# Keys laid out tile by tile, with more transposes given to the DMA and a new order of instructions

## The chip, the cores and the metric

The kernel runs on one core of a Trainium2 chip. Its time is the device time of one execution in microseconds (us); before the change the median of three runs is 264.69 us (263.86 to 265.36). The profile is one execution, recorded by the hardware profiler; its span is 262.8 us from the first instruction to the last. The engines are called by what they do: TensorE (PE in the profile; its weight loads are PEld) multiplies matrices, VectorE (DVE) and ScalarE (ACT) compute elementwise and read its results, GpSimd (POOL) computes elementwise on the on-chip memory, and SyncE (SP, with its queue SPq) issues transfers. Each engine takes its instructions strictly in the order in which the program has them.

## The reference, cut to what matters

Attention over 4 batches, 8 heads, 768 positions and 64 elements per head. Three heads see all earlier positions; the other five see only the last 64 positions and the first 4. The attention output is then the input of a gated feed-forward block.

```python
scores = (1 / sqrt(D)) * q @ k^T                      # [4, 8, 768, 768]
stream_keep = causal & (is_sink | in_win)             # n_sink 4, window 64
mask = where(is_retrieval, causal, stream_keep)       # heads 0, 2, 6 are retrieval
a = exp(where(mask, scores, -1e9) - max); a = a / sum(a)
x = (a @ v) as [3072, 512]                            # batch and position by head and element
g = x @ w_gate; val = x @ w_val                       # 512 -> 1536
out = (g * sigmoid(g) * val) @ w_out                  # 1536 -> 512
```

## The kernel before

All matrices are float16 with float32 sums. Positions go in tiles of 128; a *pair* is two tiles of one batch (12 pairs, 24 tiles), and the feed-forward block works on *groups* of four tiles (6 groups). Per pair the kernel loads q, k and v (512 KB each), casts them, and turns q and k so that the head's elements lie on the partitions. Per tile it computes scores (line 530), their exponentials (540), masks (548), the product with the values (560) and the division (577), and turns the result, `xb`, into `xt`. Per group and block of 128 columns there are a gate product and a value product (761), a tanh (767), two VectorE steps (771, 778), and per tile an output product in three parts (790).

Turning is done in two ways, and three constants say from which pair or tile on the second is used:

```python
XBAR = 12    # outputs: tiles 12 to 23 by a transposing DMA, earlier ones on TensorE
XQK = 5      # queries: pairs 5 to 11 by DMA
XK = 8       # keys:    pairs 8 to 11 by DMA
```

Keys on TensorE take eight transposes into a PSUM tile (line 423) and a copy out of it (lines 175 and 177, through a helper); by DMA they take four transfers for a pair:

```python
kT = [const.tile([128, 4, S], FH, name=f"kT{n}") for n in range(2)]   # by batch: element, head pair, position

def dmak(n, j):                                   # line 408; j: even or odd positions
    b, pi = QP[n]
    for m in range(2):                            # m: which tile of the pair
        at = pi * 256 + m * 128 + j * 64
        nc.sync.dma_start_transpose(
            out=kT[b % 2][:, :, at:at + 64],
            in_=hqs[n][m * 64:(m + 1) * 64, 1, j].rearrange("p r x -> p (r x)"))

def transposes(n, w):                             # w: 0 queries, 1 keys
    ...
    for j in range(2):
        for p in range(4):
            nc.tensor.transpose(tr[:, p, :, j, :] if w else tr[:, j, p, :],
                hqs[n][:, w, j, p // 2, (p % 2) * 128:(p % 2 + 1) * 128], ident)

def evack(n, x, ps):
    b, pi = QP[n]
    copy(T_ev[n, 2][x], kT[b % 2][:, ps, pi * 256:(pi + 1) * 256],
         trs[n, 1][:, ps].rearrange("c p m j n -> c p (m j n)"))
```

An output tile takes four transposes and a copy, or one transfer; a query pair takes two transfers of `hqz`, which holds the cast queries among zeros:

```python
def xtranspose(t):
    ...
    if t >= XBAR:
        nc.sync.dma_start_transpose(              # line 587
            out=xts[g][:, :, n * 128:(n + 1) * 128], in_=xb.rearrange("p a b d -> p (a b d)"))
        return
    ...
    for p in range(4):
        nc.tensor.transpose(tr[:, p, :], xb[:, p].rearrange("p a d -> p (a d)"), ident)   # line 593

def dmaq(n, j):                                   # line 400
    nc.sync.dma_start_transpose(
        out=qT[n % 2][:, :, :, j].rearrange("c s p n -> c (s p) n"),
        in_=hqz[:, j].rearrange("p s a x -> p (s a x)"))
```

The order of all instructions is planned ahead: `ORDER` is a string with two characters for each task, `WAYS` says which engine does a task that several could do. A number from 3700 on in `ORDER` is no task: it puts that many matmuls of the identity with itself there, which fill a gap of TensorE (`warm`).

```python
for number in P.order():
    if number < P.FILL:
        P.tasks[number].run()
    else:
        warm(number - P.FILL)
```

Of the kernel before, what the change touches and what calls it, by code (L numbers as in the profile page):

```python
# [13 lines left out]


ORDER = (
    "08020409001L1Mxp1T1U011W1N1Oy21Y1V0B251X1Z0A1Q051a1t061p031u1q261b1c1d072D1P2G1e0C1n1f1g271R1r28"
    "1o1S0i2E2F1i1j1h1k2I1K1v0D0E0F2J2A2H1l2K2C1s2j0o2k2L1m1y1w1x1z222M0j112120232V0H2B24292N2O0p109T"
    "2W2p2q2P2r122Z9U2X2a2b2s2t2Y9J159K2Q132u2R2v2S2c2T9W9V3Q9d2d2e2U0I2x369L9e0G2h9X9f2y9M2i9N0l9n9o"
    "169i9j2w303W9k9p319q3X3G3H9r2z3R9g9h9s2m3Y9v2l9t9u9w1B0m9O9P3D0k3E9Q9R9S9Y9Z2n3Z3A9a3M323a3B9l3C"  # L20
    "331E9m2oACAD3b3c0s34359b9c0K3FAHAI3eAE3p3d370OAJ0JAM0q0L3I3J3f38391FAN3t189xAO2f3uAK494FAL9y4H3K"
    "9z0n3g3wAP3L3xAQA24G3j3kA3A7190t3TA84s3h3y3NA43S3i4z504A3l3mA01H4I4J413VA13n42AR3o0MA93q3U3O3PAW"
    "3z0R3v43AS44A5A61I403r4N3s2g45464OAUAT4KAV0rAX47480z1C4LAY4D0N4rAZAFAa0uAG5b4W4a4bBPBQBRBS4qAvAw"
    "BT4M4Q4RAA4E4CBFAB0x1D4B0v1J4dAxAyBGBH0wAz4eBU174x4m5i4gBVBWBe0y1G4S5jBX141ABhAb4cBY4h4P4y54Ac0Q"
    "4T0WAd55AeBfBg4UBK51Ag4V0b4X4iBi52BABB0P4j5aBo5758Ah4f0X0UBC5FBNBp4t5JBLAiBM4k530V5K0T5L5Z595ABD"
    "BOAj6m0S5MBE4lB55hBq5N4Y4Z4n4uB60aBIAlBJ5B6756Am5P5Q5CBrBs5D5EBZBa6AAk4w5g0hB76EAn6F5R5SAoB85s5t"
    "66BjBbBm5O6B4o5kAf4v4p5l5mAq656D7T5H5I5G5T5UAr5u5v5VBk5wAsBlBnB0At6C5W5cBc5XB1626G5d5nB97a5e0Z6u"
    "BdB35YCw5x7UB2B4CD6H0d5o6JCx5f6KCG6kCE5yBt6l6S6VAu6WCy5z69607V68CF7XBuBv6IBw6L6Y6Z6r0YCH616qCN6s"
    "5p5qCcByCdCI63ApCeCQ6M6hCOCP8gCJ0g7b6O7WCSCT6NCRBzC0C17RCU8f6PCfCgCVCW6b6c6XCL5r7SCr6n6Q6TCKCs6t"
    "CMD66RD70c6v6aBx7YC36d6wCmD8CzD0C47Z7n0fCu6x6e7oCtCvCXCYCZCnCo6f6y796g0e81CpCq8364Ca6z7kD96U6jDA"  # L30
    "6i6o75767lC57374D1C67mCbD2D37172DkDlDmEOD47q8h7C6p7pDaEPEQ7DChCiD57r707zCj82877ECkCl777F7G7H7u78"
    "E480E5C8C27K7LERES7IDb86DcC9Du7y7A7B7JDd7xE6CACB847cDp7MDe7d7eDBDCDnDqDr8588DD7N7sC7DoDx7tDv89Ds"
    "DwDtEEEFEGDE8BDFDfDg8CDy8K8D7O7PDh8ADiDjE77f7gE88N8O8cEHDG8Q8RDzEIE0E9E1EA7QEB8E8FEJEK8i7wEL7h8e"
    "8mCCDHDIDJE27i7jDL8TE38UDMDN8l7vECDODPEx8GEDFHEMFI8dFJ8j8kEyEzENDQDR8H8ZDVDWF2DXDYDZDSDT8P8nF08o"
    "F1ET8p8IFgF3DUF5F4FA8q8rF68J8MF7EUF8EVEWF99194Fh8LEs8VEY95FiFBFCFD978SEZEaEtEv8WEu8X98FKEwFEDK8v"
    "8wFL99Eb8Y8aFjFMFNFF8b8s8x968tFO8uFkEXEd8yFREeEnFGEoFeEp8z9092Ec9C9DEfEgFSFTEqErEh9A9BEi9E9FFbFU"
    "FVFc9GEjEk9H93FdFWFfFXFZFP9IFYGPFaFQElGSGjFlFmGQGRGkGlFnFoEmGTG5G6GmGZGaG7GKFqGLGMFpGnGbFrFsFtG8"
    "GtGuG9GUGVGWGNGOFvGvGcGyGdH1FwGwGzH0FxGxH2FyGAGBGCGFGGFuGIGHGJGeGfGDG0GgGEGhGiGXGoGYGpFzG1G2G3Gr"
    "H3H4GqGsH5G4H8H9HAHDH6H7HBHCHEHFHIHGHHHJHKHLHM"
)  # L40
WAYS = (
    "000000000000000000000000000000000000000000000000000000000000001020021121222210112011001222001011"
    "001000000000000000000000000001101200212120111100100000000010000000000100022220000101000001000000"
    "110000100000000011012221020010100000100000000010100000000000000002202120010000000100000020010000"
    "010000001000122120100010010010000000001010000000000000001221221200010000000000000000000102021221"
    "000000100000000001000100000000012002200220000001000000000001200000000000000000020200000000100000"
    "000000000021010221110000001001000000000001000000000010022010000000010000000000011000100100000000"
    "000000000000000000000000000000000000000000000000000000000000000000000000000000000000100000000010"
    "000000000000000000000000000000000000000000000000000000000000000000000000000000000000000000000000"
    "000000000000000000000000000000000000000000000000000010000000000000010000000000000000000000000000"  # L50
    "000000000000000000000000000000000000000000000000000000000000000000000000000000000000000000000000"
    "000000000000000000001000000000000000000000000000000000000000000000000000000000000000000000000000"
    "000010000100001000000"
)
# [51 lines left out]
def kernel(  # L106
# [66 lines left out]
    def copy(task, dst, src):  # L173
        if task.way == "ACT":
            nc.scalar.copy(out=dst, in_=src)  # L175
        else:
            ENG[task.way].tensor_copy(out=dst, in_=src)  # L177
# [179 lines left out]

    XBAR = 12  # L360
# [52 lines left out]

    def transposes(n, w):

        ring = "gv" if w and n < 2 else "tr"
        if w:
            tr = buf(ring, [128, 4, 2, 2, 64], FH, "tr")
        else:
            tr = buf(ring, [128, 2, 4, 128], FH, "tr")  # L420
        for j in range(2):
            for p in range(4):
                nc.tensor.transpose(
                    tr[:, p, :, j, :] if w else tr[:, j, p, :],
                    hqs[n][:, w, j, p // 2, (p % 2) * 128:(p % 2 + 1) * 128], ident)
# [482 lines left out]
```

The softmax here doesn't subtract the row's maximum and nothing guards it: scores larger than these inputs give would overflow.

## Time and profile before

| | |
|---|---|
| time, median of 3 | 264.69 us (263.86 to 265.36) |
| span of the profiled execution | 262.8 us |
| TensorE clock granted | 0.996 |
| moved by DMA | 41.23 MB, 157 GB/s in the mean |
| first real transpose on TensorE starts | 5.78 us |
| last matmul ends about | 258.3 us |

In the lists, an instruction stands with its line, its engine and `out<-in`; x is how often it comes, then follow its busy time, the mean of one in ns, and the time the engine stood idle just before it with what ended that wait. A matmul's mean contains its way through the array, which the next one overlaps, so that the means of small matmuls add up to more than they cost. The 40 slices of the page are 6.6 us each and count busy tenths. A line of the chain is work that nothing else could have replaced on the way to the last instruction, followed back from it.

### The profile page before, as it was taken

To read this page: it belongs to the slowest core of one execution; us is meant where nothing else is said; L and a number is where in the kernel's file an instruction comes from. 1 tells how busy PE (TensorE), PEld (TensorE's weight loads), DVE (VectorE), ACT (ScalarE), POOL (GpSimd) and SP (SyncE) were. 2 spreads that over 40 slices of the span, in tenths; PEclk is the share of its full clock that TensorE was granted. 3 is DMA by queue.
4 is the path that set the end of the run, shared out by engine and by line. 5 is a ranking of instruction groups with operands and counts; after the bars stand their busy time and mean duration, and the time that the engine had idled before them with its cause. 6 is when DMAs were issued, how large, how long until landed. Compare 5 with 4: busy or idle time off the path is not lost.

```text
span 262.8 us, 4993 instructions
## 1 busy us (share of the span) xinstructions
PE 247.6 (94%) x1890; PEld 141.3 (54%) x1890; DVE 174.6 (66%) x357; ACT 140.3 (53%) x216; POOL 89.7 (34%) x123
## 2 busy tenths in 40 slices
PE   7878899899999989999899999999999999999993
PEld 7656775565555655545455555554555554444441
DVE  3887988989777569857398747527459365557421
ACT  2777797686548467758286754722363522323100
POOL 5468769462268073261330033800315100000000
PEclk9999999999999999999999999999999999999998
DMA  6999999994999979794972342253212221211143
GB/s 185 302 275 329 326 312 310 319 361 124 219 290 291 228 196 147 184 237 101 263 119 60 43 99 58 55 120 69 62 40 62 62 58 40 47 36 41 28 94 81
DMA packets 75192, 41.23 MB, mean 157 GB/s; under 512 B 27552, under 2 KB 70560, under 8 KB 75168
## 3 DMA queue, kind: packets, MB, share of 16 engines
q1 hardware_dynamic: 75088, 40.78, 63.9%
q8 instruction: 15, 0.25, 0.4%
q10 hardware_dynamic: 80, 0.13, 0.2%
q14 instruction: 9, 0.07, 0.1%
HBM read 28.31 MB, written 6.29 MB: 132 GB/s over the span
## 4 chain that ended last, share of the span: by engine, by line
PE 67%; DMA 12%; DVE 6%; SPq 6%; POOL 3%; ACT 3%; issue 2%; POOLq 0%; DVEq 0%; ACTq 0%
PE gv L761 36%; PE o_ps L790 20%; PE sc L530 6%; DMA raw<-in_q_dram 6%; PE av L560 4%; DMA qT<-hqz 3%; DMA raw<-in_k_dram 3%; SPq L309 3%; SPq L400 2%; DVE sil L771 1%; DVE e L548 1%; ACT e L540 1%; POOL hq L177 1%; DVE h L778 1%; POOL e L548 1%
## 5 line engine op out<-in xcount | busy, mean ns | idle before, releaser
L540 ACT ACTIVATE e<-sc 128x1024 f16<-128x1024 f32 (+4 forms) x71 | 62.2, 879 | 41.0 <-PE sc L530 40.4
L761 PE MATMUL gv<-xt,wv_sb 128*128 128x512 f16 (+1 forms) x304 | 73.0, 368 | 1.0 <-DVE sil L771 1.0
L761 PE MATMUL gv<-xt,wg_sb 128*128 128x512 f16 (+1 forms) x304 | 72.9, 368 | 0.6 <-POOL wg_sb L177 0.6
L771 DVE SCALAR_TENSOR_TENSOR sil<-sig,gv 128x512 f32<-128x512 f32 (+1 forms) x76 | 49.4, 655 | 32.8 <-ACT sig L767 32.4
L790 PE MATMUL o_ps<-wo_sb,h 128*128 128x512 f16 x288 | 69.7, 379 | 0.0
L767 ACT ACTIVATE sig<-gv 128x512 f32<-128x512 f32 (+1 forms) x76 | 43.0, 574 | 45.1 <-PE gv L761 44.5
L778 DVE SCALAR_TENSOR_TENSOR h<-sil,gv 128x512 f16<-128x512 f32 (+1 forms) x76 | 49.3, 656 | 24.2 <-PE gv L761 23.0
L548 POOL TENSOR_TENSOR e<-e,m 128x1024 f16<-128x1024 f16 (+1 forms) x17 | 31.8, 1873 | 54.1 <-ACT e L540 54.0
L761 PEld LDWEIGHTS <-wv_sb 128*128 128x128 f16 x304 | 28.6, 98 | 28.0 <-issue 1.3
L761 PEld LDWEIGHTS <-wg_sb 128*128 128x128 f16 x304 | 28.5, 98 | 26.3 <-POOL wg_sb L177 0.8
L790 PEld LDWEIGHTS <-h 128*128 128x128 f16 x288 | 27.3, 98 | 28.5
L530 PE MATMUL sc<-qT,kT 128*128 128x256 f16 (+1 forms) x276 | 37.5, 257 | 3.1 <-DMA qT<-hqz 2.0
L530 PEld LDWEIGHTS <-kT 128*128 128x128 f16 x276 | 24.6, 98 | 15.7 <-DMA qT<-hqz 3.0
L560 PEld LDWEIGHTS <-e 128*128 128x128 f16 x472 | 20.2, 97 | 10.0 <-DVE vt L177 1.5
L560 PE MATMUL av<-vt,e 128*128 128x65 f16 x472 | 22.5, 193 | 1.7 <-DVE vt L177 1.0
L577 DVE TENSOR_TENSOR xb<-av,rc 128x256 f16<-128x256 f32 x48 | 20.2, 423 | 1.5
L177 POOL CAST vt<-raw 64x512 f16<-64x512 f32 x21 | 13.8, 660 | 11.1 <-DMA raw<-in_v_dram 10.3
L177 POOL CAST hq<-raw 128x1024 f16<-128x1024 f32 (+1 forms) x14 | 14.8, 1058 | 6.6 <-DMA raw<-in_q_dram 5.1
L548 DVE TENSOR_TENSOR e<-e,m 128x640 f16<-128x640 f16 (+1 forms) x21 | 15.8, 754 | 1.8 <-ACT e L540 1.7
L175 ACT COPY o_sb<-o_ps 128x512 f32<-128x512 f32 x15 | 8.8, 584 | 11.6 <-PE o_ps L790 11.6
L177 POOL COPY vt<-vt 2x330 f16<-2x330 f16 x20 | 9.6, 481 | 14.2 <-PE av L560 13.6
L177 DVE COPY o_sb<-o_ps 128x512 f32<-128x512 f32 x8 | 5.5, 690 | 9.3 <-PE o_ps L790 8.0
(59 smaller groups left out, 142.0 us busy)
## 6 DMA issues: line engine op xcount, KB each, us to landing
raw<-in_q_dram SPq DMA_DIRECT2D x12, 512.0 KB, 6.9
raw<-in_k_dram SPq DMA_DIRECT2D x12, 512.0 KB, 7.4
raw<-in_v_dram SPq DMA_DIRECT2D x12, 512.0 KB, 7.4
out_dram<-o_sb SPq DMA_DIRECT2D x47, 128.0 KB, 2.4
raw<-in_moe_w_gate_dram SPq DMA_DIRECT2D x6, 512.0 KB, 8.0
raw<-in_moe_w_val_dram SPq DMA_DIRECT2D x6, 512.0 KB, 7.5
raw<-in_moe_w_out_dram SPq DMA_DIRECT2D x6, 512.0 KB, 8.5
kT<-hq SPq DMA_TRANSPOSE x16, 2.5
```

The source lines that it names most:

```text
L175: nc.scalar.copy(out=dst, in_=src)
L177: ENG[task.way].tensor_copy(out=dst, in_=src)
L530: nc.tensor.matmul(sc[c // 4][:, c % 4:c % 4 + n, :], weights, moving, start=first, stop=last)
L540: nc.scalar.activation(out=e[:, 0:n], in_=whole_sc.pop((t, u))[:, 0:n], func=AF.Exp, scale=scale)
L548: ENG[task().way].tensor_tensor(out=ev, in0=ev, in1=mm, op=ALU.mult)
L560: nc.tensor.matmul(av[:, n, 0:65], ee, vv, start=(m == 0), stop=(m == len(bl) - 1))
L577: nc.vector.tensor_tensor(out=xbs[t][:, :, odd, :], in0=av[:, :, 0:64], in1=rc.to_broadcast([128, 4, 64]), op=ALU.mult)
L761: nc.tensor.matmul(ps, wsb[:, kk, j * 128:(j + 1) * 128], xt[:, kk, c[0]:c[1]], start=(kk == 0), stop=(kk == 3))
L767: nc.scalar.activation(out=sg[g, j, c], in_=gs[g, j, c], func=AF.Tanh, scale=0.5)
L771: nc.vector.scalar_tensor_tensor(out=sl[g, j, c], in0=sg.pop((g, j, c)), scalar=1.0, op0=ALU.add, in1=gs.pop((g, j, c)), op1=ALU.mult)
L778: nc.vector.scalar_tensor_tensor(out=hs[g, j][:, c[0]:c[1]], in0=sl.pop((g, j, c)), scalar=0.5, op0=ALU.mult, in1=vs.pop((g, j, c)), op1=A ...
L790: nc.tensor.matmul(o_open[g, tt], hs[g, j][:, tt * 128:(tt + 1) * 128], wo_sb[:, j, :], start=(j == 0), stop=(j == NJ - 1))
```

## The change

Two things are done to give TensorE fewer transposes. First the keys get a layout in which one transposing DMA fills one tile of 128 positions as one contiguous piece per partition, so that a pair takes two transfers and not four. Second, the constants move: keys of pairs 5, 6 and 7 and outputs of tiles 8 to 11 now go by DMA. The new layout changes the cast of the keys, their copy out of PSUM, the copy of the first positions (sinks) and the address of a block of keys in the scores. `ORDER` and `WAYS` are planned anew, and the matmul that makes the masks for later tiles is tied behind a gate of the first group. The order before has two groups of filling matmuls (9 and 22), the new one has seven (11, 19, 16, 15, 16, 6 and 8); 40 more stand at the very start in both.

```diff
-    kT = [const.tile([128, 4, S], FH, name=f"kT{n}") for n in range(2)]
+    kT = [const.tile([128, NT, 2, 2, 128], FH, name=f"kT{n}") for n in range(2)]
@@
-    XBAR = 12
+    XBAR = 8
     XQK = 5
-    XK = 8
+    XK = 5
@@ cast
-            hqs[n] = buf("hq", [128, 2, 2, 2, 256], FH, "hq")
+            h = buf("hq", [128, 2, 1024], FH, "hq")
+            hqs[n] = [h[:, 0].rearrange("p (j r x) -> p j r x", j=2, r=2),
+                      h[:, 1].rearrange("p (k a x) -> p k a x", k=2, a=4)]
+        if kd == "k":
+            ks = slice(0, 2) if x is None else slice(x, x + 1)
+            copy(T_c[n, kd, x],
+                 hqs[n][1][:, ks].rearrange("p k a (s d) -> p k s a d", s=2),
+                 r.rearrange("p (k s r) j d -> p k s (r j) d", r=2, s=2)[:, ks])
+            return
@@
-    def dmak(n, j):
+    def dmak(n, m):
         b, pi = QP[n]
-        for m in range(2):
-            at = pi * 256 + m * 128 + j * 64
-            nc.sync.dma_start_transpose(
-                out=kT[b % 2][:, :, at:at + 64],
-                in_=hqs[n][m * 64:(m + 1) * 64, 1, j].rearrange("p r x -> p (r x)"))
+        nc.sync.dma_start_transpose(
+            out=kT[b % 2][:, 2 * pi + m].rearrange("c k r (j n) -> c (k r j) n", j=2),
+            in_=hqs[n][1][m * 64:(m + 1) * 64].rearrange("p k a x -> p (k a x)"))
@@ evack
-             kT[b % 2][:, ps, pi * 256:(pi + 1) * 256],
-             trs[n, 1][:, ps].rearrange("c p m j n -> c p (m j n)"))
+             kT[b % 2][:, 2 * pi:2 * pi + 2].rearrange("c m k r x -> c (k r) m x")[:, ps],
+             trs[n, 1][:, ps].rearrange("c p m j n -> c p m (j n)"))
@@ block
-        return kT[b % 2][:, p, kt * 128:(kt + 1) * 128]
+        return kT[b % 2][:, kt, p % 2, p // 2]
@@ the gates
+                if g == 0 and j == 3:
+                    T_mord.after.append(a)
... (ORDER and WAYS as a whole; transposes, sinks_k and the task lists follow the new layout)
```

More of the change, by code (lines that the diff above doesn't have):

```diff
@@ L16 @@
 ORDER = (
[L17 to L36, printed above, removed]
@@ L37 @@
-    "FVFc9GEjEk9H93FdFWFfFXFZFP9IFYGPFaFQElGSGjFlFmGQGRGkGlFnFoEmGTG5G6GmGZGaG7GKFqGLGMFpGnGbFrFsFtG8"
-    "GtGuG9GUGVGWGNGOFvGvGcGyGdH1FwGwGzH0FxGxH2FyGAGBGCGFGGFuGIGHGJGeGfGDG0GgGEGhGiGXGoGYGpFzG1G2G3Gr"
-    "H3H4GqGsH5G4H8H9HAHDH6H7HBHCHEHFHIHGHHHJHKHLHM"
+    "030208041L0900011Mxr1T0B1X1N1W1O1V1Uxz1Y1Z1axw1n0C2526281o0A1r1d1K1P2D272H1e1t1u2E1p0E0D2I2G2K2J"
+    "1b2F1c0F1q1Qxv1f1s1R1S1g2V2j2W0j1i211h1j0p1v1w1x1y2C1k2p2q0H2r2A2k1z2Lxw1l2M1m292N2O2X15202P2s2B"
+    "2t2Z2axm232b162Y2x2y0k2c249Z2d2e2h2i2Q2u2v0I9j2R362S2T2U9k3Q9lxo309o9a319b053W2g9p073X9m9n9q180G"
@@ new lines @@
+    "3D3E3Y06229y9z3R3A9r3B9s3Z9c3M3a2w9d9t0q9u9eA02l2z2m32333b0i199f9g2o9w0m9v343c3G9x35A1A2109F3H9h"
+    "1E9i3C9G112n370o3e9K0l129H0K9L3p13389M9P9Q9I3I9S9J3f9U9R3d0J3j3k9V3FAI9W9T3t3u391B0L3T493U9N9X3J"
+    "4F3K3w9Y2fA80n4H9OAD3S4GAJAK3L3x1H3hA9AE3NAF4A4I3i3lAN3z3V3vAS0s1FAAAL3m3g3n404JAM3o413OAGAOAPAT"
+    "420O3q3y43440t4N4q4O1IA3453PAH4K3r464LAV0M3sAU47A44WAWA54Z0r0u4a1C48AB4CA6A7AC4M4f0N4BBLAQ0v4o4y"
+    "4g4c4xARBMBN4S4T4b4p4EBOBP4dBaBb4v4wBf4l4QBQBc0QBgBh4PBRB6Bd0PBS4D4eB7Be4RB152530z0w4UB24X0x5WB8"
@@ new lines @@
+    "B94VBA4rBBBC4zB3504hBT17B45556BU1J545DBD4YBiBE0RB55G4iBj5H5I0y1D4s0U1ABG4j4k4nBk4m5V5cBF14BHAX5d"
+    "AY5MAw4tBI1G4uAZ5N5X5eAz5O5fAa5P51595AAcBl570SAdAeAb585B5EAxAyB0Af5C5JAr0b5K5L5Q5RBn63Bm6B5b5g5S"
+    "5h5TAhAiBV5ZBoBWAsAt5FAj5iAk5r0TBXBY5Y5s5j5k5UAmBJBKAn5o625a615p0XD2D35lAoAl6A5q68BZApC969D4Au5m"
+    "CACE5tAv7S5uBpBqCJ5vCBCH6i5yCFCG0V677RCI6I665wCiCK6J0WCj0h65CMCL5z6F6G7TCNAq6g6HBr0a6qCC0YCD8b6C"
+    "Cl6h64CkCm6DCnCoBsAgCpCq5n6pCr6OCY6E7PCZ6X6YCaCsCtD0Bu6R6S6TCx6oCy8d5xCzD1Bv6UBw6n6VCd6K0ZCb6L6l"
@@ new lines @@
+    "6d6r7XBx6M6PCe0g6sCuByCTCU6NBzCc6u6Q6ZCf6v6W7OC0C1606a7N7VD5D66b6k6e7Q6zBt6c7W70CO6jC2Cv6xC46w6f"
+    "Cw756yC57U0d8c6m788e79CVC6CWC7C87v7B6t71CPCQ7C0f72Dy83DvDwCX730c7Y7ZDxDzE5CRCg7GE6E77HCSE0Ch7gE8"
+    "D774E1E27h76E9EKEL7a7ED87tEM7bDR7ADS7FDUD9Dl7c7uDTDm7dDVDA7j7kDnDoDpE37iDb0e7e7mE47DDcDd7zDq81Dg"
+    "Dh7q7l7nDi8a7w8280848Z8i85DCC3Dr7o7r777pDjDk8788DD7I7JDsDEDF7KDB7L897f7x8Y8f8G8MDWDHDt8g8NDX868C"
+    "DuDY8AEAEN8BEB8P7MEFEO8hEG8QDZDI8D8EECDa8J8KEHDJDK7sEIEJ8HEDDe8FEoEEF3DfEpEq8VDMDN7yFXFYEr8O8L8R"
@@ L40 @@
+    "8S8m8nDOF48TFZ8j8kEsF5FDFEFFFaFbDG8UDL8x8IEt8l938WEuFGEvFI8t94FH8r8sFcFdDPFeDQ9091EwEPEQExFJFK8p"
+    "8qFfEj8uERFgFNESEkF6F7ETEUEV8o8v988w8zFOFP92ElFLEWEXFSFQFTFM958y99FU9AEy9BEYFR96EzF1EZ8XF0979CF2"
+    "F89D9EEaEbEcF9FAFVFBEmFWEeEfEgEnEhFCG6GkG7G8GlG9GmGAGnEdGLGMGoGpGNGsFhGQFiFjGqGrGtGRGSFkGOGPGGGH"
+    "GuGvGwFlGaFmGJGIGKGbGxFnFoFpGcGdGeG1FrFqGTG2GyFsFtGfGgG3GBFuGhGUFwFxGCGVGDGEGFG4G5FvGWFyGYGiFzG0"
+    "GXGZGjEiGzH0H1H4H5H6H9H2HAHBH3H7H8HEHFHGHCHDHHHI"
 )
 WAYS = (
-    "000000000000000000000000000000000000000000000000000000000000001020021121222210112011001222001011"
@@ L43 @@
[L43 to L47, printed above, removed]
@@ L48 @@
-    "000000000000000000000000000000000000000000000000000000000000000000000000000000000000100000000010"
-    "000000000000000000000000000000000000000000000000000000000000000000000000000000000000000000000000"
-    "000000000000000000000000000000000000000000000000000010000000000000010000000000000000000000000000"
-    "000000000000000000000000000000000000000000000000000000000000000000000000000000000000000000000000"
-    "000000000000000000001000000000000000000000000000000000000000000000000000000000000000000000000000"
@@ L53 @@
-    "000010000100001000000"
+    "000000000000000000000000000000000000000000000000000000000000002222222222022200211200210211100111"
+    "011000000000101000000000000000100211222010101101100000000000000000000110121220201101000000000000"
+    "100000100000000011012220220000000000000000000010000100100000000002220000110100000000000011000000"
+    "100000010002212020000000000000000002100000000000000001012121000000100000001001000001001200220000"
+    "000000000000210001001000000220020202200000000010000000020000100000000000012022110000001000000010"
@@ new lines @@
+    "000000110122120100000000000000001000000000000000201020111000000100000000000100001000000000000000"
+    "000000000000000000000000000000000000000000000000000000000000000000000000000000000000000000000000"
+    "000000000000000000000000000000000000000000000000000000000000000000000000001000000000000000000000"
+    "000000000000000000000000000000000000000000000000100001000010000100000000000000000000000000000000"
+    "000000000000000000000000000000000000000000100000000000000000000000000000000000000000000000000000"
@@ L54 @@
+    "000000000000000000000000001000010000000000000000000000000000000000000000000000000000000000000000"
+    "10000000001000000"
 )
@@ L378, in cast @@
         if n not in hqs:
-            hqs[n] = buf("hq", [128, 2, 2, 2, 256], FH, "hq")
+            h = buf("hq", [128, 2, 1024], FH, "hq")
[7 more added lines that the diff above has]
+            return
         js = slice(0, 2) if x is None else slice(x, x + 1)
         copy(T_c[n, kd, x],
-             hqs[n][:, "qk".index(kd), js].rearrange("p j r (k d) -> p k r j d", d=64),
+             hqs[n][0].rearrange("p j r (k d) -> p k r j d", d=64)[:, :, :, js],
              r[:, :, js].rearrange("p (k r) j d -> p k r j d", r=2))
@@ L416, in transposes @@
         ring = "gv" if w and n < 2 else "tr"
[L417 to L420, printed above, removed]
+        tr = buf(ring, [128, 4, 2, 2, 64] if w else [128, 2, 4, 128], FH, "tr")
         for j in range(2):
             for p in range(4):
-                nc.tensor.transpose(
-                    tr[:, p, :, j, :] if w else tr[:, j, p, :],
-                    hqs[n][:, w, j, p // 2, (p % 2) * 128:(p % 2 + 1) * 128], ident)
+                if w:
+                    nc.tensor.transpose(tr[:, p, :, j, :], hqs[n][1][:, p // 2, p % 2 * 2 + j],
+                                        ident)
+                else:
+                    nc.tensor.transpose(
+                        tr[:, j, p, :],
+                        hqs[n][0][:, j, p // 2, (p % 2) * 128:(p % 2 + 1) * 128], ident)
         trs[n, w] = tr
@@ L435, in evack @@
         copy(T_ev[n, 2][x],
-             kT[b % 2][:, ps, pi * 256:(pi + 1) * 256],
-             trs[n, 1][:, ps].rearrange("c p m j n -> c p (m j n)"))
+             kT[b % 2][:, 2 * pi:2 * pi + 2].rearrange("c m k r x -> c (k r) m x")[:, ps],
+             trs[n, 1][:, ps].rearrange("c p m j n -> c p m (j n)"))
     def sinks_k(b, m):
-        T = kT[b % 2].rearrange("c p (t j n) -> c p t j n", j=2, n=64)
-        for cs, ps in ((slice(0, 128), slice(2, 4)), (slice(0, 64), slice(1, 2))):
-            copy(T_sk[b, m], T[cs, ps, m, :, 0:NSINK // 2], T[cs, ps, 0, :, 0:NSINK // 2])
+        T = kT[b % 2].rearrange("c t k r (j n) -> c t k r j n", j=2)
+        for cs, k, r in ((slice(0, 128), slice(0, 2), 1), (slice(0, 64), slice(1, 2), 0)):
+            copy(T_sk[b, m], T[cs, m, k, r, :, 0:NSINK // 2], T[cs, 0, k, r, :, 0:NSINK // 2])
     def sinks_v(b, m):
@@ L641, in tasks_of_pair @@
             T_ev[n, 2] = [P.lands(P.add(
-                f"dk{n}.{j}", ["SP"], (lambda n=n, j=j: dmak(n, j)),
-                deps=cs["k"] + older)) for j in range(2)]
+                f"dk{n}.{m}", ["SP"], (lambda n=n, m=m: dmak(n, m)),
+                deps=cs["k"] + older)) for m in range(2)]
             P.uses(first, "hq", *T_ev[n, 2])
@@ L651, in tasks_of_pair @@
             if w:
-                for x, ps in enumerate(cut):
+                for x, ps in enumerate([slice(1, 4, 2), slice(0, 4, 2)] if n < 2 else cut):
                     evs.append(P.add(f"evk{n}.{x}", ["ACT", "DVE"],
```

## The prediction

> **What bounds the kernel now.** I read the page's table of engines first, then its 40 slices, then the chain that ended last, then five stretches of my own choosing, and last the waits and the shapes of the instructions.
>
> ```profile
> PE 247.6 (94%) x1890; PEld 141.3 (54%) x1890; DVE 174.6 (66%) x357; ACT 140.3 (53%) x216; POOL 89.7 (34%) x123
> ...
> PE   7878899899999989999899999999999999999993
> ...
> DMA  6999999994999979794972342253212221211143
> ...
> PE 67%; DMA 12%; DVE 6%; SPq 6%; POOL 3%; ACT 3%; issue 2%; POOLq 0%; DVEq 0%; ACTq 0%
> ```
>
> TensorE is busy 94% of the span and is 67% of the chain; everything else in the chain lies in the first half. The five stretches say where TensorE is not busy (columns: start and end, length, busy time with instruction count of TensorE, its weight loads, VectorE, ScalarE, GpSimd; then clock, DMA share, GB/s):
>
> ```profile
> 5.78:30.00 24.22, 19.15 (x241) 15.39 (x239) 19.90 (x50) 18.74 (x32) 14.89 (x23) 1.00 1.13 303
> 30.00:60.00 30.00, 27.83 (x286) 18.76 (x286) 26.82 (x59) 22.19 (x34) 20.73 (x27) 1.00 1.10 329
> 60.00:93.00 33.00, 32.46 (x250) 18.14 (x247) 24.80 (x52) 19.72 (x28) 13.62 (x14) 1.00 1.01 225
> 93.00:130.00 37.00, 35.54 (x265) 19.59 (x266) 26.07 (x55) 23.72 (x36) 16.42 (x21) 1.00 0.81 183
> 130.00:258.30 128.30, 128.26 (x806) 64.96 (x804) 73.93 (x139) 53.47 (x87) 20.22 (x21) 1.00 0.32 66
> ```
>
> From 130 us to the last matmul TensorE has no hole (128.26 of 128.30), so any TensorE instruction that goes away before then, and any hole closed before then, moves the end by its own length unless a new wait eats it. From 93 to 130 us 1.5 us are open, from 60 to 93 us 0.5, from 30 to 60 us 2.2, and from 5.78 to 30 us 5.1. After the last matmul there are 4.5 us of evacuation and store, which no part of the change touches.
>
> The wait list names two holes behind a transposing DMA, and the timeline places them at 93.23 us (0.78 us) and 128.72 us (1.20 us):
>
> ```profile
> POOL hqz L177 <- DMA qT<-hqz: 11.3, 2, 7.7
> ...
> PEld L530 <- DMA qT<-hqz: 3.0, 2, 1.7
> PE sc L530 <- DMA qT<-hqz: 2.0, 2, 1.2
> ```
>
> The columns are the total, the number of waits and the longest. The DMA queue has waits of its own:
>
> ```profile
> SPq L587 <- DVE xb L577: 19.1, 4, 8.9
> ```
>
> SyncE stands on an output tile that VectorE has not written yet, and all that is queued behind it stands too.
>
> **What the Trainium skill says.** "TensorE: Matmul & The Clock Gate", section "Back-to-back issue gap", gives 55.6 ns from one matmul to the next at 128 columns and 215.7 at 512. The trace agrees: eight transposes start at 33.61 us and the next group at 34.06 (56 ns each), and four 512-column matmuls take 0.86 us. So the listed mean of 219 ns is a latency, not what a transpose costs the engine. "VectorE: DVE Perf Modes", section "The three transpose paths", gives 390 ns to TensorE and 1309 ns to the DMA for 128x128: the DMA path is slower and only pays where nobody waits. The trace agrees in sense: 2.5 us from issue to landing for the key transfers, 4.2 us for the queries. "DMA: Bandwidth & Descriptors", section "Anatomy of one DMA — SWDGE (gpsimd) path", says that a semaphore wait happens on the issuing sequencer before dispatch; the 19.1 us above is that. "TensorE: Matmul & The Clock Gate", section "Part 1: The HAM clock gate (the "warmup" mystery)", has the array's clock follow how busy it has recently been; this is what the filling matmuls are for, and the trace shows the clock at 1.00 in every stretch.
>
> **The change part by part.** The shapes that it concerns (time, mean of one, idle before):
>
> ```profile
> L423 PE MATMUL tr<-ident,hq 128*128 128x128 f16 x104 | 8.1, 219 | 1.7 <-DVE qT L177 0.6 <-POOL hq L177 0.4 <-DVE kT L177 0.4
> ...
> L593 PE MATMUL xtr<-ident,xb 128*128 128x128 f16 x48 | 4.6, 219 | 1.0 <-DVE xb L577 0.7 <-DVE qT L177 0.3
> ...
> L175 ACT COPY xt<-xtr 128x512 f16<-128x512 f16 x7 | 4.1, 581 | 1.1 <-PE xtr L593 1.1
> ...
> L177 DVE COPY kT<-tr 128x1024 f16<-128x1024 f16 x4 | 2.7, 685 | 0.0
> ...
> L175 ACT COPY kT<-tr 128x1024 f16<-128x1024 f16 x2 | 2.0, 1010 | 2.4 <-PE tr L423 2.4
> ```
>
> And the page's list of DMA issues (number, then the median us from issue to landing):
>
> ```profile
> kT<-hq SPq DMA_TRANSPOSE x16, 2.5
> qT<-hqz SPq DMA_TRANSPOSE x14, 4.2
> xt<-xb SPq DMA_TRANSPOSE x12, 2.4
> ```
>
> (1) Keys of pairs 5, 6 and 7 leave TensorE: 3 x 8 = 24 transposes. Outputs of tiles 8 to 11 leave it: 4 x 4 = 16. Together 40 x 56 ns = 2.2 us of TensorE, all of it between about 47 and 103 us (the last transpose of a key starts at 90.3, of an output at 102.1), ahead of the full stretch. This lies on the path that sets the end: -2.2 us.
>
> (2) Their evacuations go: in the order before, keys 5 and 6 on VectorE (2 x 0.69), key 7 on ScalarE (1.01), outputs 9 on VectorE (0.42) and 8, 10, 11 on ScalarE (3 x 0.58). That is 1.8 us of VectorE and 2.8 us of ScalarE. Between 60 and 130 us VectorE is busy 50.9 of 70 us and ScalarE 43.4, so most of it is slack: 0 to -0.3 us, counted as none.
>
> (3) Transposing DMAs. Before: 16 + 14 + 12 = 42. After: keys of 7 pairs x 2 = 14, queries 14, outputs 16: 44. SyncE takes 1.2 to 1.35 us to issue one, whether of 64x512, 128x512 or 128x1024 elements, so a key transfer that is twice as large should issue in about 1.25 us, and the four pairs that already went this way free 8 x 1.25 = 10 us of SyncE. Landing I estimate at 2.5 to 3.5 us, between the 2.4 of an output transfer, which moves the same 128 KB, and the 4.2 of a query transfer with twice that. SyncE is not on the path after 130 us. Worth in time: 0 by itself.
>
> (4) The order, decoded task by task. The start is different: load g1 is the first weight, ninth in the row, where g0 was the sixth; the mask matmul and its nine VectorE copies (2.9 us at 9.3 us before) move behind the first gates; the zeroing of hqz moves from GpSimd to VectorE. Filling matmuls inside the order rise from 31 to 91. At 56 ns the 60 more are 3.4 us of TensorE, but each group stands where the plan expected TensorE to have nothing, and the kernel before idles 5.1 us in just that stretch. So they mostly replace idle time. The first sixteen loads, the last of which lands near 32.5 us before (where GpSimd's wait for it ends), hold the same kinds in both orders (four q, four k, three v, five weights), and with 303 to 329 GB/s moved all the way to 60 us neither order gets more data sooner. Estimate for the start: +0.3 us, with 1.5 either way.
>
> (5) The two holes behind query transfers. In the new order query transfer 6 stands behind the output transfer of tile 9, and the output transfers of 10 and 11 stand ahead of query transfer 7: four more places where SyncE waits on VectorE, in return for the time freed under (3). I counted what TensorE has between the cast of query 7 and its first use: 12 blocks of 0.86 us and about 1.2 us of small ones, 11.6 us, against two or four issues (2.6 to 5.2 us) and 4.2 to 7.8 us of landing. Tight, not broken. Of the 2.0 us I expect 0.4 to be gained.
>
> Sum: -2.2 + 0.3 - 0.4 = -2.3 us; 264.7 - 2.3 = 262.4 us.
>
> **The rivals.** (A) The start gets worse. The 60 more fills are a statement of the plan that TensorE will be idle there by 3.4 us more; if unplanned holes stay as they are (5.1 us to 30 us), the start loses up to 3.4 us and the end is 264.7 - 2.6 + 3.4 = 265.5. For it: TensorE works in order, so a fill that comes when real work is ready delays it. Against: the new order has the keys of pair 1 one load earlier and queries of pair 2 two loads earlier, and real work ahead of the first gate is larger. (B) A key or query transfer lands late: loads and transposes share one queue, and up to 7.8 us to land has been seen. Two holes of 2 us in place of the two of 1 give 264.7 - 2.2 + 2 = 264.5; a chain of late tiles could give 267. For it: GpSimd already stands 11.3 us behind query transfers. Against: between the cast of key 5 and its first use the order has 19 blocks of 0.86 us and several small ones, over 16 us. (C) All holes after 60 us close (2.0 us) and the start keeps its length: 264.7 - 2.2 - 2.0 = 260.5. (D) Nothing measurable, because TensorE's saved time was under a wait anyway: 264.7. Against: the transposes lie in stretches that are 93 to 98% busy.
>
> **Range and chances.** The transposes are sure to 0.3 us; start (1.5) and holes (1.2) are not. I take 259.5 to 265.8 us as the range for 8 in 10, wider upward for A and B. Faster by over 2% means below 259.4 us: C and a better start at once, 0.10. Slower by over 2% means above 270 us, a late chain: 0.05. Within 2%: 0.85.
>
> **What would show it.** Step 1: 80 and 32 transposes instead of 104 and 48, TensorE's real work shorter by 2.2 us, and still no hole from 130 us on. Step 3: 14 key transfers, issue near 1.25 us, landing 2.5 to 3.5. Step 4: fills plus holes up to 30 us near what holes and fills were before; if A is right, the 60 to 258 us part is shorter by over 2 us and the start longer by over 2. Step 5: waits of the scores on DMA below 2.0 us in sum. I am wrong in kind if waits on kT or xt transfers appear before 130 us with more than 2 us, or if VectorE, at 89% from 30 to 60 us, becomes the wait before the gates.

## The result and the profile after

| | before | after |
|---|---|---|
| time, median | 264.27 us (263.71 to 265.36) | 260.62 us (260.14 to 261.08) |
| ratio | 1 | 0.9857, 95% interval 0.9817 to 0.9897 |
| span of the profiled execution | 262.8 us | 259.0 us |
| last matmul ends | 258.3 us | 254.3 us |

The time before is the median of four executions here; the 264.69 us ahead of the prediction is that of the first three. The change gains 3.65 us, where 2.3 were predicted. The page of the kernel after, engines, slices and chain:

```profile
PE 248.4 (96%) x1910; PEld 142.9 (55%) x1910; DVE 178.5 (69%) x360; ACT 134.1 (52%) x210; POOL 86.2 (33%) x122
...
PE   7979999998998999999999999999999999999992
...
DMA  7999999966985799999569875551012320111243
...
PE 82%; DMA 6%; DVE 5%; SPq 3%; issue 1%; ACT 1%; POOL 0%; DVEq 0%; POOLq 0%; ACTq 0%
```

TensorE has gone from 67% to 82% of the chain, and DMA from 12 to 6%. The busy time of TensorE has not fallen, because the 60 more filling matmuls count as busy. The five stretches of the kernel after, with the columns as in the prediction:

```profile
5.78:30.00 24.22, 22.39 (x305) 18.85 (x303) 19.52 (x55) 17.04 (x29) 12.24 (x20) 1.00 1.15 308
30.00:60.00 30.00, 29.37 (x299) 20.47 (x298) 28.02 (x63) 24.33 (x37) 23.17 (x30) 1.00 0.96 273
60.00:93.00 33.00, 31.44 (x250) 17.22 (x249) 26.78 (x48) 18.49 (x30) 13.46 (x16) 1.00 0.88 219
93.00:130.00 37.00, 37.00 (x253) 19.61 (x252) 25.36 (x48) 24.70 (x42) 16.75 (x20) 1.00 0.99 217
130.00:254.60 124.60, 123.85 (x770) 62.35 (x769) 76.17 (x145) 47.28 (x74) 15.89 (x17) 1.00 0.38 83
```

From 30 to 60 us the open time fell from 2.2 to 0.6 us, from 93 to 130 us from 1.5 to 0; from 60 to 93 us it rose from 0.5 to 1.6. The last stretch ends 0.3 us after the last matmul, so that 0.4 us are open in it, where there was no hole before. What TensorE waits for in the whole execution, total, number and longest:

```profile
PE gv L770 <- DVE h L787: 1.5, 2, 0.8
...
PE av L569 <- DVE xb L586: 0.7, 2, 0.4
PE gv L770 <- DVE sil L780: 0.6, 1, 0.6
```

No wait for a DMA is left on TensorE. The two waits for `h` are new; they lie at 64 and 80 us and are for VectorE, for the products that free a PSUM buffer of the gates. They are what opened from 60 to 93 us. One of the waits for `xb`, 0.4 us, is the hole behind 130 us. Shapes and DMA issues:

```profile
L602 PE MATMUL xtr<-ident,xb 128*128 128x128 f16 x32 | 3.1, 219 | 0.4 <-DVE xb L586 0.3
L430 PE MATMUL tr<-ident,hq 128*128 128x128 f16 x40 | 3.1, 219 | 0.7 <-POOL hq L177 0.7
L427 PE MATMUL tr<-ident,hq 128*128 128x128 f16 x40 | 3.1, 219 | 0.0
```

```profile
xt<-xb SPq DMA_TRANSPOSE x16, 2.5
kT<-hq SPq DMA_TRANSPOSE x14, 2.8
qT<-hqz SPq DMA_TRANSPOSE x14, 3.3
```

Queries land in 3.3 us where they took 4.2, and keys in 2.8 though each transfer is twice as large.

**How the runs are compared.** Busy time hides what a short matmul costs, so each profiled execution is split by a count of its matmuls: each is given the time from its start to the next one's start when nothing waits (30 ns for 65 columns, 56 for 128, 109 for 256, 162 for 384, 216 for 512, all read off dense stretches of the traces). Their sum, without fills, is the *work*; what remains of the time up to a point is *lost*. The last matmul ends at work plus lost. Each row is one execution, so some tenths between two rows mean little: the wait at 80 us is 0.70 us after and 0.26 us in the same kernel without its fills.

| profiled execution | work, us | lost by 30 us | by 60 | by 93 | by 130 | in all | last matmul ends |
|---|---|---|---|---|---|---|---|
| before | 237.6 | 14.6 | 17.7 | 18.5 | 20.4 | 20.7 | 258.3 |
| after | 235.4 | 14.3 | 15.6 | 17.5 | 17.6 | 18.9 | 254.3 |
| layout alone, old order | 237.6 | 14.6 | 17.6 | 18.7 | 19.5 | 19.7 | 257.3 |
| both moves, old order | 235.4 | 14.3 | 17.1 | 20.1 | 29.3 | 29.5 | 264.9 |
| keys moved, old order | 236.3 | 14.6 | 17.3 | 20.3 | 23.1 | 24.1 | 260.4 |
| outputs moved, old order | 236.7 | 14.6 | 17.7 | 18.8 | 27.6 | 28.4 | 265.1 |
| new order, nothing moved, first | 237.6 | 14.4 | 15.7 | 19.8 | 20.0 | 20.6 | 258.2 |
| new order, nothing moved, later | 237.6 | 14.4 | 15.7 | 16.6 | 16.8 | 17.3 | 255.0 |
| new order, keys moved | 236.3 | 14.4 | 15.7 | 17.3 | 17.2 | 17.8 | 254.1 |
| new order, outputs moved | 236.7 | 14.5 | 15.7 | 17.3 | 17.5 | 17.9 | 254.7 |
| after without fills | 235.4 | 14.3 | 15.6 | 17.1 | 17.6 | 18.0 | 253.4 |
| after, VectorE mended twice | 235.4 | 14.2 | 15.6 | 15.8 | 16.7 | 17.0 | 252.4 |

Of the 4.0 us between the last matmuls, 2.2 are work, 0.2 are gained by 30 us and 1.9 from 30 to 60 us, and 0.4 are given back after that: 1.1 more are lost from 60 to 93 us, 1.8 less from 93 to 130 us, and 1.0 more to the end. From 30 to 60 us the kernel before had these four waits:

```profile
30.29 0.60 PE L761 MATMUL gv<-xt,wv_sb 128*128 128x256 f16 x4 [0.99 <-DVE sil L771]
...
41.18 1.04 PE L761 MATMUL gv<-xt,wg_sb 128*128 128x512 f16 x4 [0.55 <-POOL wg_sb L177]
...
48.63 0.42 PE L560 MATMUL av<-vt,e 128*128 128x65 f16 x8 [0.70 <-DVE vt L177]
...
50.34 0.61 PE L423 MATMUL tr<-ident,hq 128*128 128x128 f16 x8 [0.44 <-DVE kT L177]
```

They are for four different products of VectorE and GpSimd: a step of the gates, a cast of weights, a cast of values and a copy of keys. After the change one wait of that size is left there:

```profile
38.40 0.60 PE L770 MATMUL gv<-xt,wv_sb 128*128 128x256 f16 x4 [0.58 <-DVE sil L780]
```

The questions to the chip were: does the gain belong to the moves or to the order, and do the fills matter?

### The profile page after: what moved, and what is told of

Read it like the earlier page. It is cut to its first block, busy times and chain, and to the rows that moved or that the text cites. A ratio compares the mean times of both kernels' runs of the same rounds, so it can differ in the third digit from the quotient of the medians.

```text
span 259.0 us, 5044 instructions
## 1 busy us (share of the span) xinstructions
PE 248.4 (96%) x1910; PEld 142.9 (55%) x1910; DVE 178.5 (69%) x360; ACT 134.1 (52%) x210; POOL 86.2 (33%) x122
## 4 chain that ended last, share of the span: by engine, by line
PE 82%; DMA 6%; DVE 5%; SPq 3%; issue 1%; ACT 1%; POOL 0%; DVEq 0%; POOLq 0%; ACTq 0%
PE gv L770 43%; PE o_ps L799 23%; PE sc L539 8%; PE av L569 5%; DMA raw<-in_q_dram 3%; SPq L309 2%; DMA raw<-in_k_dram 2%; DVE h L787 1%; DVE vt L177 1%; PE xtr L602 1%; ACT e L549 1%; DVE sil L780 1%; DVE e L557 1%; DVE xb L586 1%; PE warm L285 1%
## 5 line engine op out<-in xcount | busy, mean ns | idle before, releaser
L787 DVE SCALAR_TENSOR_TENSOR h<-sil,gv 128x512 f16<-128x512 f32 (+1 forms) x76 | 49.2, 655 | 18.8 <-PE gv L770 17.3
L770 PEld LDWEIGHTS <-wv_sb 128*128 128x128 f16 x304 | 28.9, 98 | 28.4 <-issue 1.0
L799 PEld LDWEIGHTS <-h 128*128 128x128 f16 x288 | 27.6, 98 | 30.2
L557 POOL TENSOR_TENSOR e<-e,m 128x1024 f16<-128x1024 f16 (+1 forms) x15 | 28.5, 1903 | 23.7 <-ACT e L549 18.2
L175 ACT COPY o_sb<-o_ps 128x512 f32<-128x512 f32 x13 | 7.6, 584 | 29.0 <-PE o_ps L799 27.9
L586 DVE TENSOR_TENSOR xb<-av,rc 128x256 f16<-128x256 f32 x47 | 19.8, 424 | 1.6
L177 POOL CAST hq<-raw 128x1024 f16<-128x1024 f32 (+1 forms) x12 | 12.0, 1001 | 17.9 <-DMA raw<-in_k_dram 12.1
L557 DVE TENSOR_TENSOR e<-e,m 128x640 f16<-128x640 f16 (+1 forms) x23 | 15.2, 667 | 2.7 <-ACT e L549 2.6
L177 POOL CAST vt<-raw 64x512 f16<-64x512 f32 x22 | 15.4, 700 | 5.0 <-DMA raw<-in_v_dram 3.4
L177 POOL COPY vt<-vt 2x330 f16<-2x330 f16 x18 | 8.4, 464 | 22.9 <-PE av L569 22.4
L574 DVE RECIPROCAL rc<-av 128x4 f32<-128x4 f32 x48 | 8.4, 176 | 9.9 <-PE av L569 9.7
```

The source lines that it names most:

```text
L557: ENG[task().way].tensor_tensor(out=ev, in0=ev, in1=mm, op=ALU.mult)
L574: nc.vector.reciprocal(out=rc, in_=avs[t, odd][:, :, 64:65])
L586: nc.vector.tensor_tensor(out=xbs[t][:, :, odd, :], in0=av[:, :, 0:64], in1=rc.to_broadcast([128, 4, 64]), op=ALU.mult)
L770: nc.tensor.matmul(ps, wsb[:, kk, j * 128:(j + 1) * 128], xt[:, kk, c[0]:c[1]], start=(kk == 0), stop=(kk == 3))
L787: nc.vector.scalar_tensor_tensor(out=hs[g, j][:, c[0]:c[1]], in0=sl.pop((g, j, c)), scalar=0.5, op0=ALU.mult, in1=vs.pop((g, j, c)), op1=A ...
L799: nc.tensor.matmul(o_open[g, tt], hs[g, j][:, tt * 128:(tt + 1) * 128], wo_sb[:, j, :], start=(j == 0), stop=(j == NJ - 1))
```

## The experiments

In the names of tasks, `tr5.1` is the transposing of the keys of pair 5 on TensorE and `evk5` its copy, `dk5` its transfers, `xtr8`, `xe8` and `xdma8` the same for the output of tile 8, `dq` a query transfer. The runs were made on several chips; kernels are compared by their ratio to the kernel before, measured on the same chip.

### Layout alone, and both moves in the old order

The layout alone keeps the order before:

```diff
-    XBAR = 8
-    XK = 5
+    XBAR = 12
+    XK = 8
     (ORDER, WAYS: those of the kernel before)
```

> The order of the kernel before with the new key layout alone: keys of pairs 8 to 11 take two transfers for a pair and not four, nothing else moves. Theory (the layout only frees SyncE, which is not on the path): 264.3 us, within 0.6 us of before, 8 key transfers of 1.25 us to issue each, the two holes behind query transfers (0.78 and 1.20 us) stay within 0.5 us in sum. Rival (SyncE's queue was what made the query transfers late): the two holes close and the time falls by about 2 us to 262.3.

Measured: 263.71 us, ratio 0.9967 (0.9954 to 0.9979), 0.9 us less, between both theories. The two holes behind query transfers did close to less than 0.1 us, as the rival had it: SyncE's queue had made these queries late. But two holes of 0.32 and 0.54 us, ahead of gates that wait for VectorE, opened at 61 and 84 us.

Both moves without a new order:

```diff
     (constants and layout as after; ORDER, WAYS of the kernel before, with)
-    tr5.1 tr6.1 tr7.1, xtr8 xtr9 xtr10 xtr11
-    evk5 evk6 evk7, xe8 xe9 xe10 xe11
+    dk5 dk6 dk7 (two each), xdma8 xdma9 xdma10 xdma11   # each where its copy stood
```

> The order of the kernel before with both constants moved and the new layout: each transpose and its copy is taken out where it stood, and the transfer stands at the copy's place. No other task moves. Theory M (moves pay by themselves, the new order pays the rest): TensorE loses 2.2 us of transposes and the hole of 0.44 us ahead of the query transposes of pair 4, which waited for the copy of the keys of pair 5: 261.6 us, transfers waited for by scores no more than 2.0 us in sum as before. Rival R (without a new order the transfers give the gain back): more than 1.5 us of new waits on kT or xt or for loads that stand behind them, 263.5 us or more.

Measured: 273.36 us, ratio 1.0316 (1.028 to 1.0352): 8.8 us slower, though TensorE does 2.2 us less work. Theory M has fallen. Part of the loss is not waiting: behind the longest hole the clock is at half for 3.4 us (last section), which is 1.7 us of work not done, by estimate. TensorE's waits in this run:

```profile
PE gv L770 <- DMA xt<-xb: 3.1, 1, 3.1
PE sc L539 <- DMA qT<-hqz: 3.0, 1, 3.0
...
PE av L569 <- POOL vt L177: 1.5, 1, 1.5
```

How such a wait comes about can be read in SyncE's timeline (start, length, line, transfer; line 408 is a query, 596 an output, 309 a load, 823 a store):

```profile
82.86 3.71 SPq L408 DMA_TRANSPOSE qT<-hqz  x1
86.67 1.86 SPq L596 DMA_TRANSPOSE xt<-xb  x1
89.04 0.37 SPq L309 DMA_DIRECT2D raw<-in_k_dram  x1
89.52 1.40 SPq L823 DMA_DIRECT2D out_dram<-o_sb  x2
90.96 1.35 SPq L408 DMA_TRANSPOSE qT<-hqz  x1
```

and in what the other engines did then:

```profile
95.57 0.61 PE L539 MATMUL sc<-qT,kT 128*128 128x256 f16 x4 [2.98 <-DMA qT<-hqz]
95.63 0.83 POOL L177 CAST hqz<-raw 128x512 f16<-128x512 f32 x1 [9.05 <-DMA qT<-hqz]
...
100.78 0.37 PE L569 MATMUL av<-vt,e 128*128 128x65 f16 x7 [1.54 <-POOL vt L177]
```

The output of tile 8 was put between the two halves of the queries of pair 6. The second half went out at 90.96 us, 1.9 us later than in the kernel before, and landed at 95.5. The scores waited 2.98 us for it. GpSimd waited 9.05 us for the same landing, because `hqz` is one buffer and the next queries may not be cast into it sooner; behind that cast, and behind one of keys that waited 1.96 us for a key transfer, stood the copies of sinks for which the value products then waited 1.54 us. The kernel before had no room for this: in its trace the queries of pairs 5, 6 and 7 land 0.54, 0.05 and 0.15 us before their first use. In the kernel after it is 4.5, 4.5 and 3.2 us.

### Which move, and is it SyncE's order?

```diff
     (order before, layout and constants)
+    keys run:    XK = 5, XBAR = 12        outputs run: XK = 8, XBAR = 8
```

> The order before, new layout, keys of pairs 5 to 7 by DMA at the place of their copies, outputs 8 to 11 still on TensorE. Taken with the new layout alone at 263.7 us. Theory O (the outputs make the loss, because SyncE stands still for each of them until VectorE has written it): TensorE loses 24 transposes (1.3 us) and the 0.44 us hole, gets one hole of about 1 us ahead of the first scores of tile 10 because the key transfers of pair 6 stand before a query transfer: 263 us. Rival K (the key transfers make the loss): 268 us or more.

Measured: 267.22 us, ratio 1.0089 (1.0061 to 1.0118): a loss as well, short of rival K's 268 us and far from theory O. The hole ahead of tile 10 came (1.39 us), and one of 1.69 us ahead of the scores of tile 13, behind a query transfer.

> The order before, new layout, outputs of tiles 8 to 11 by DMA at the place of their copies, keys 5 to 7 still on TensorE. Theory O: most of the 8.8 us that both moves together lost, with holes of about 3 us ahead of the first scores of tile 13 and about 3 us ahead of the first gate of group 2: 269 to 272 us. Rival K: 264 us or less, since 16 transposes (0.9 us) are saved.

Measured: 271.94 us, ratio 1.027 (1.024 to 1.03), a time as theory O has it. The holes are 3.7 us ahead of the first gate of group 2, waiting for the output of tile 11, and 1.7 and 0.8 us behind queries.

```diff
     (both moves in the old order; SyncE's queue alone)
-    dq5.0 ... dk6 dk6 dq5.1      dq6.1 xdma8 ... dq6.0      dk9.0 load q9 dk8.1 xdma11
+    dq5.0 ... dq5.1 dk6 dk6      dq6.1 ... dq6.0 xdma8      xdma11 dk9.0 load q9 dk8.1
```

> Both moves in the order before, every engine's order as in the run of both moves, but in SyncE's queue the key transfers of pair 6 stand after the query transfers of pair 5, the output of tile 8 after the query transfers of pair 6, and the output of tile 11 ahead of a key transfer, a load and a key transfer of later pairs. Theory S (SyncE's order made the loss): the holes ahead of tile 10 (1.1 us), of tile 13 (3.0 us) and of group 2's first gate (3.1 us) shrink by more than half, 273.4 falls to 267 to 269 us. Rival (the transfers are slow in themselves or TensorE meets them too early, whatever their place): less than 2 us better, 271.5 us or more.

Measured: 270.98 us, ratio 1.0214 (1.0169 to 1.026), 2.7 us better than with the first queue by the ratios (1.0316 less 1.0214, of 264.7; taken together the two intervals allow 1.2 to 4.2). That is more than the rival allows and less than theory S asked for, so SyncE's queue is a cause of the loss, and three swaps do not settle it. The profiled execution of this run took 272.7 us, well above its median, and serves for a sketch only: the hole ahead of group 2's gate shrank to 0.4 us, those ahead of the scores of tiles 10 and 13 stayed at 0.9 and 2.3 us, and the one ahead of value products, behind copies on GpSimd, grew from 1.5 to 2.7 us.

### The new order without the moves

```diff
     (order after)
-    XBAR = 8
-    XK = 5
+    XBAR = 12
+    XK = 8
     first:  tr, evk, xtr, xe at the places of dk and xdma
     later:  tr three, xtr two TensorE tasks later, each copy one more
```

> The new order with both constants set back: keys 5 to 7 and outputs 8 to 11 are turned on TensorE at the place where their transfers stood. Theory M: the kernel after plus 2.2 us of transposes plus 0.3 to 1 us of waits for their copies: 262.9 to 263.8 us, with the stretch from 30 to 60 us still about 1.5 us better than before. Rival R2 (the new order is worth nothing without the moves): 264.3 us or more.

Measured: 264.65 us, ratio 1.0006 (0.999 to 1.0021). By the letter this is rival R2. But its stretch to 60 us was as good as after (lost 15.7), and TensorE's waits said where the rest went:

```profile
PE xtr L602 <- DVE xb L586: 1.7, 2, 1.5
PE av L569 <- DVE e L557: 1.4, 1, 1.4
```

A transfer may stand in SyncE's queue before its input is there; a transpose at the same place makes TensorE stand. So the run had measured where the work was put back, not the order, and was repeated with later places:

> The new order with both back on TensorE, as in the first run of this kind, but each set of transposes two or three tasks later, so that TensorE does not meet it before its input is there. Theory P: the kernel after plus 2.2 us and little more, 262.8 to 263.3 us, and the holes of 1.48 and 1.38 us of the first run gone. Rival Q: 264.3 us or more, as in the first run.

Measured: 262.08 us, ratio 0.9906 (0.9886 to 0.9926): better than theory P had it. Its waits for the gates' buffers:

```profile
PE gv L770 <- DVE sil L780: 0.8, 2, 0.6
PE gv L770 <- DVE h L787: 0.3, 1, 0.3
```

The order, with the layout, is worth 2.5 us without the moves. The moves add 1.3 us to that (0.9906 to 0.9857; the intervals just overlap), not the 2.2 us of work which they save. The profiled executions point the same way: lost time in all is 17.3 us here and 18.9 after, and the same gates wait 2.1 us there against 1.1 here; their last matmuls are 0.7 us apart, so the 1.3 us is good to about half a microsecond.

### Each move in the new order

```diff
     (order after; later places as above)
+    e9:  XBAR = 12, XK = 5   # outputs back on TensorE
+    e10: XBAR = 8,  XK = 8   # keys back on TensorE
```

> The new order with the keys of pairs 5 to 7 by DMA as in the kernel after, and the outputs of tiles 8 to 11 back on TensorE, each set of transposes two of TensorE's tasks behind the place of its transfer and its copy one more. Theory P (order and moves add up: the returned work costs its own length): the kernel after plus 16 x 56 ns = 0.9 us, 261.5 us, up to 262.2 with one short wait. Rival Q (the new order is only good with all moves, because its VectorE and ScalarE have no room for the copies): 263 us or more, with new holes behind VectorE.

Measured: 260.59 us, ratio 0.9855 (0.9835 to 0.9876), the same as after, below theory P's 261.5 and far from rival Q. Sending the outputs of tiles 8 to 11 by DMA brings nothing that can be measured here.

> The new order with the outputs of tiles 8 to 11 by DMA as in the kernel after, and the keys of pairs 5 to 7 back on TensorE, three tasks behind the place of their transfers. Theory P: the kernel after plus 24 x 56 ns = 1.3 us, 261.9 us, up to 262.6. Rival Q: 263.5 us or more.

Measured: 261.26 us, ratio 0.9884 (0.9865 to 0.9903), 0.6 us below theory P's 261.9. Keys are worth 0.3% of the time on top of the outputs (0.9884 to 0.9857) and 0.5% without them (0.9906 to 0.9855), 0.7 to 1.3 us; outputs 0.2% without the keys (0.9906 to 0.9884) and nothing with them. The intervals of neighbours overlap, so only the two ends are sure.

### The fills

```diff
     (order after)
-    warm(11) warm(19) warm(16) warm(15) warm(16) warm(6) warm(8)
```

> The kernel after without the 91 filling matmuls inside the order (the 40 at the very start stay). Theory F (they only take time in which TensorE would wait): 260.6 us within 0.6, holes up to 30 us grow by about the 4.9 us that the fills took, clock still 1.00. Rival A (they delay real work): up to 3 us faster. Rival H (they hold up the clock): the granted clock before 30 us falls below 0.97 and the time rises by 1 us or more.

Measured: 260.21 us, ratio 0.9836 (0.9816 to 0.9857), which cannot be told from after's 0.9857. The first stretch of this run:

```profile
5.78:30.00 24.22, 18.05 (x217) 14.10 (x217) 20.39 (x55) 17.12 (x29) 12.10 (x20) 1.00 1.16 309
```

TensorE is busy 4.3 us less than after, and no less work is done by 30 us (15.7 us in both); the clock is 1.00 with or without. Theory F holds, and rivals A and H have fallen. The prediction took these fills to be there for the clock; at holes of this length (1.4 us at most) they were not needed for it.

### A version that beats both

The waits for VectorE in the kernel after are a matter of its order. This is the one at 64 us in the kernel after:

```profile
61.66 1.79 DVE L557 TENSOR_TENSOR e<-e,m 128x1024 f16<-128x1024 f16 x1
...
63.38 0.67 DVE L787 SCALAR_TENSOR_TENSOR h<-sil,gv 128x512 f16<-128x512 f32 x1
...
64.10 1.89 PE L770 MATMUL gv<-xt,wg_sb 128*128 128x512 f16 x8 [0.80 <-DVE h L787]
```

The mask (line 557) is needed only by value products 9 us later, and the product behind it (line 787) frees the buffer for which the gate waits.

```diff
     (after without fills; VectorE's order)
-    nm8.1 mask9.0 stt2 1.6.0          mask11.0 nm9.0 sv1.3 cq6.0 stt2 1.4.0     sv0.2 stt1 0.0.0 sk0.4
+    nm8.1 stt2 1.6.0 mask9.0          mask11.0 nm9.0 stt2 1.4.0 sv1.3 cq6.0     stt1 0.0.0 sv0.2 sk0.4
     second run, in addition:
-    sk0.4 stt1 0.0.256                stt1 1.11.0 cx6.1.1 nm11.0 cx6.0.1 stt2 1.11.0
+    stt1 0.0.256 sk0.4                stt1 1.11.0 stt2 1.11.0 cx6.1.1 nm11.0 cx6.0.1
```

> The kernel after without the 91 fills, and three swaps in VectorE's order: a copy of sinks behind a tanh's first product, a mask behind a product that frees a PSUM buffer, and such a product ahead of a copy of sinks, an output's division and a query cast. If the three holes (0.59, 0.80 and 0.26 to 0.70 us) are paid at the end one to one: about 1.5 us less than without the fills, 258.7 us. If VectorE is itself the bound there and only swaps one wait for another: 260.2 us.

Measured: 259.65 us, ratio 0.9807 (0.9784 to 0.983), between the two expectations. The holes at 64 and 80 us closed; the third did not, for where 0.59 us had been there were 0.78 us at 39 us; one of 0.99 us at 93 us was new.

> The kernel after without the 91 fills, with the three swaps of the run before, and two more in VectorE's order: the key sinks of the second tile in line behind the product that frees the buffer, and a product ahead of a cast that waits for a load. If the two holes that the first swaps left behind (0.78 us at 39 us and 0.99 us at 93 us) close and nothing else opens: 258.7 us or less. If the waits only move on again: 259.6 us.

Measured: 258.97 us, ratio 0.9799 (0.9776 to 0.9822), 5.3 us under the kernel before, measured beside it. The middle stretches of this run:

```profile
60.00:93.00 33.00, 32.94 (x261) 18.17 (x260) 26.27 (x50) 20.23 (x33) 14.47 (x17) 1.00 0.96 222
93.00:130.00 37.00, 36.53 (x248) 19.13 (x247) 25.80 (x50) 23.61 (x41) 15.67 (x18) 1.00 0.91 217
```

From 60 to 93 us nothing is open now, where the kernel after had 1.6 us; 0.5 us came back at 97 us, where a gate waits for a cast of queries on VectorE. The median stays 0.3 us above the 258.7 that was expected.

## Why the prediction held, and which term was too small

**Step 1, the work: right; what it is worth: too much.** 80 and 32 transposes stand where 104 and 48 stood, and the work is 237.6 less 235.4, 2.2 us. But not all of it arrives at the end: in the new order both moves bring 1.3 us. The rule that an instruction less "moves the end by its own length unless a new wait eats it" was right, and the sum left its second half out. The old order shows such a wait: without the eight transposes of the keys of pair 5 (0.45 us) the value products right behind them waited 1.15 us where they had waited 0.70. "Still no hole from 130 us on" did not come true in the profiled execution, with 0.4 us open behind VectorE.

**Step 2, the copies: right in size.** With them in the new order (the later places) TensorE waits no longer than without.

**Step 3, the transfers: right.** 14 key transfers, median issue 1.27 us, median landing 2.8 us. "1.2 to 1.35 us to issue one" is the usual case only: of the 14 query transfers of the kernel before four took 2.1 to 5.2 us, of those after none took over 1.5. "Worth in time: 0 by itself" was a little low: the layout alone gained 0.9 us.

**Step 4, the start: right to 30 us, and too short.** Real work by 30 us is 15.5 us before and 15.7 after, so the fills and rival A cost nothing. But the step stopped at 30 us. The first view had named 2.2 us open from 30 to 60 us, and no term of the sum used them; the new order gained 1.9 us just there. In every run with the new order lost time by 60 us is 15.6 to 15.7 us, and in every run with the old one 17.1 to 17.7.

**Step 5, the holes behind transfers: the wrong sign of the rest.** The DMA waits of 2.0 us went entirely, but after 60 us as a whole 0.4 us more was lost instead of 0.4 less, through the waits for VectorE. The prediction had named this as a way to be wrong in kind, "if VectorE ... becomes the wait before the gates", and it came true: the gates wait 2.1 us for VectorE, where they had waited 1.0. It came mostly at 64 and 80 us; from 30 to 60 us, where the prediction looked for it, it is 0.6 us.

So the mis-sized term is the order, put at 0.3 less 0.4 us, that is 0.1 us of gain; with the layout it measures 2.5 us, about 0.9 of which the layout brings alone in the old order. The moves, put at 2.2, measure 1.3. That the total came out within 1.4 us is in part luck, since the two errors have opposite signs. Rival C names nearly the measured time, 260.5 us, also by luck: its holes after 60 us did not close in sum, and the gain came from 30 to 60 us, where it had none. **Rival B** described what the moves do in the old order, and was too mild: put at the places of the copies, they lose 8.8 us. "Tight, not broken" held for the new order only because it gives queries 3 to 4.5 us of slack.

What stays open: which rearrangement closes the four waits from 30 to 60 us; no run took that stretch apart. `ORDER`, `WAYS` and the place of the mask matmul changed together, and the new order was never run with the old layout, so the 2.5 us are not divided among these. How much of the 8.8 us is SyncE's queue is not known beyond the about 2.7 us of three swaps.

## What to carry to other kernels

A transfer that takes work off the bound engine is only free if the queue that issues it has slack: before moving it, list for every transfer behind it when it lands and when it is first used, and where that is a tenth of a microsecond, plan anew. When work is put back or taken away in an in-order program, the place decides as much as the work: the same transposes two or three tasks later were 2.6 us better. Once the bound engine is faster, read its waits again and look at the order of the engine that it now waits for; two rounds of swaps on VectorE brought another 0.4% here (0.9836, without the fills, to 0.9799).
